# A Fourier mixing layer beside an MLP: rows copied once more inside DRAM by chunks, row tiles loaded right behind their stores, and another order of loads and VectorE work around blocks 2 and 3

## The chip, the cores and the metric

The kernel runs on one core of one Trainium2 chip. The metric is the device time of one execution in microseconds. A measurement has several executions; the time quoted is their median.

## The reference

The input x has 2048 rows (S) of 640 columns (D); the MLP has 1536 hidden columns (F). All is float32.

```
xn  = (x - mean) / sqrt(var + 1e-5)                      # each row
y_A = Cr @ (xn @ Wr.T) - Ci @ (xn @ Wi.T)                # DFT over columns, then rows; real part
y_B = gelu(xn @ w1 + b1, approximate) @ w2 + b2
out = x + y_A + y_B
```

Cr, Ci (2048 x 2048) and Wr, Wi (640 x 640) are inputs, the matrices of the transform.

## The kernel before, in words

**Precision.** Every operand of a matmul is split into a high part (ScalarE rounds it to fp32r, line 180) and a low part (VectorE subtracts, line 183). A product is three matmuls: high by high, high by low, low by high (lines 301 to 303, or 319 for the first layer of the MLP). A matmul of 128x128 by 128x512 comes every 0.227 us at full clock.

**Stages, in order of time.** The rows are cut into four blocks of 512 (t = 0 to 3) and the hidden columns into 12 units of 128.

1. Block 0 runs through the MLP in a loop over 12 units: `hidden` (15 matmuls), `gelu`, `output` (15 matmuls). Beside it, `background(i)` loads the rows of blocks 2 and 1 in chunks of 128, normalises them (`ln_stats`, `ln_scale`, `ln_apply`), stores them to the DRAM tensor `xs`, and loads them back in another layout (`load_z`, pieces of 640 bytes) for VectorE's 32x32 transposes. From these come the "forms" of a Winograd-like scheme (`make_forms`).
2. Blocks 1 and 2 go together: `pair(k)`, six times, multiplies combinations of W1 ("pieces", `make_pieces`) by combinations of the two blocks (`window`). The units of block 2 are kept in the DRAM tensor `gs` (`keep`). Beside each pair, `beside_pair(k, at)` does other work; `at` names a place within the pair, and the places come in the order 2, 5, 6, 3, 7, 4. This work finishes block 0, and prepares the matrices Wr and Wi for later (`load_w`, `turn_w`, `prep_w`, whose results are stored to `wits`).
3. The outputs of block 2, fourteen steps `p`: `output(g)`, then the split of the unit that is used two steps later (`split_unit`, its tile loaded by `load_unit` from `gs`), then `between(p)`. It finishes block 1 (`finish`, with adds on GpSimd), normalises chunks 12 to 15 (block 3) and loads them as `z3`, transposes and splits them (`transpose_z`, `prep_xt`), and prepares W1 anew (`prep_w1`, `load_w1`), in the order of the list `AGAIN`, into places that fall free (`open_place`).
4. Block 3 runs through the MLP as block 0 did. Beside it, `fourier_step(i)` builds the Fourier part's first operand from normalised rows: `build(k)`, k = 0 to 7, at i = k + 2. `load_xr(k)` brings the rows of a build: two tiles of 128 rows, each of 32 rows from each quarter of `xs`. For k below 4 the results (`xab`, 1,280 KB, and `xc`, 896 KB) are stored to DRAM too (`forms_ab`, `forms_c`).
5. The Fourier part: products over the sequence, then over the columns, to the end.

**Order.** The program is scheduled by hand: each engine runs its instructions in the order in which they are written, and waits where an operand or a place isn't ready. Nearly all DMAs are issued by SyncE's queue (SP), so a DMA that waits holds up all DMAs written behind it. A step's two waits on SP that matter here: `load_z` reads what `ln_apply` has stored, and `load_xr(k + 2)` writes rows that `build(k)` has read.

**Places.** `PLACES` names tiles that hold W1 and W2, then forms, then W1 again: "xab2" holds units 4 and 5 of W1, "xab3" units 6 and 7. In stage 3 "xab2" first holds `xo(1)` (the rows of x to which block 1's output is added) and "xab3" holds units 3 to 7 of `gs`.

Of the kernel before, what the change touches and what calls it, by code (L numbers as in the profile page):

```python
# [10 lines left out]
F32 = mybir.dt.float32  # L11
# [4 lines left out]
P = 128  # L16
# [9 lines left out]
def kernel(  # L26
# [65 lines left out]
        return stack.enter_context(tc.tile_pool(name=name, bufs=1, side=side, reuse_waits="tile"))  # L92

    dram = ctx.enter_context(tc.tile_pool(name="dram", bufs=1, space=bass.MemoryType.DRAM))
    xs = dram.tile([S, D], F32, name="xs")

    gs = dram.tile([NF, P, TB], F32, name="gs")

# [153 lines left out]
    def load_z(z, t):  # L252

        v = rows_of(xs, t)
        for q in range(Q):
            nc.sync.dma_start(z[q * B : (q + 1) * B], v[:, :, q * DQ : (q + 1) * DQ])
# [8 lines left out]
    W1, W2, w1r, w2r = {}, {}, {}, {}  # L265


    AGAIN = (0, 1, 2, 3, 8, 9, 10, 11, 4, 5, 6, 7)

    def load_w1(i, eng=nc.sync):  # L270

# [132 lines left out]
    def put_away():  # L404
        for f in stores:
            f()
        stores.clear()
# [157 lines left out]
    def load_xr(k):  # L565
        if k >= len(builds):
            return
        h, c = builds[k]
        xr[k] = []
        if k in (0, len(builds) - 1):  # L570
            n = 2 if k else 0
            A["xcp", n] = place(f"xc{n}{n + 1}", (P, 2, 2, 7 * P))
        for half in range(2):
            if k == len(builds) - 1:

                r = A["xcp", 2][:, 1, half, :D].bitcast(F32)
            else:
                r = row_places[:, (2 * k + half) % NC]
            s0 = (half * NS // 2 + h * NK + c) * B
            for q in range(Q):  # L580
                nc.sync.dma_start(r[q * B : (q + 1) * B], xs[q * SQ + s0 : q * SQ + s0 + B])  # L581
            xr[k].append(r)

    def build(k, what="abc"):
# [117 lines left out]
    def background(i):  # L702

        if i == 0:
            ln_apply(0)
            ln_apply(1)
            A["rows_b"] = zo_tile("rows_b", (P, NC, D))
            for c in range(2 * NC, 3 * NC):
                load_x(c, home=A["rows_b"])
        if i == 1:  # L710
            ln_apply(2)
            ln_apply(3)
            for c in range(NC, 2 * NC):
                load_x(c)
        if i == 2:
            for c in range(2 * NC, 3 * NC):
                ln_stats(c)
        if i == 3:
            ln_scale(NC)
            for c in range(2 * NC, 3 * NC):  # L720
                ln_apply(c)
            ln_stats(4)
            ln_stats(5)
        if i == 4:
            Z["b"] = zo_tile("z_b")
            load_z(Z["b"], 2)
            ln_stats(6)
            ln_stats(7)
            ln_scale(NC)
            for c in range(NC, 2 * NC):  # L730
                ln_apply(c)
        if i == 5:
            Z["a"] = as_z(row_places)
            load_z(Z["a"], 1)
        if i == 6:
            new_forms()
            make_forms("b", "vb0", "vb1", "ob0")
        if i == 7:
            make_forms("a", "ua0", "ua1", "va0", "va1", "oa0")
        if i >= 8:  # L740
            (ua, va), (ub, vb) = ((Z[k][:, :, : 2 * B], Z[k][:, :, 2 * B : 4 * B]) for k in "ab")
        if i == 8:
            add(ub, ub, ua, ALU.subtract)
            make_forms("b", "t10", "t11")
            add(vb, vb, ub, ALU.subtract)
        if i == 9:
            add(ua, vb, ua, ALU.subtract)
            add(va, va, vb, ALU.subtract)
            turn_x("t20", "b")
            turn_x("t21", "b")  # L750
            load_xo(0)
# [86 lines left out]
    def finish(t, *es):  # L838
        for e in es:
            add_block(xo[t], e, oacc[t][e], f"ot{t}_{e}", bias=b2c[:, e : e + 1])  # L840

    def store_sums(t):
        for k, (c0, c1) in enumerate(YCOLS):
            nc.sync.dma_start(ys[k][t], xo[t][:, :, c0:c1])
# [3 lines left out]
    def beside_pair(k, at):  # L848

        if k == 0:  # L850
            if at == 5:
                make_forms("a", "t30", "t31")
            if at == 6:
                make_forms("a", "t40", "t41")
                load_w(0, 0)
                load_w(1, 0)
            if at == 7:
                finish(0, 0, 1, 2)
            if at == 4:
                finish(0, 3, 4)  # L860
            return
        j = k - 1
        if at == 2 and k > 1:
            prep_w(j - 1, 2)
        if at == 5:
            if k > 1:
                put_away()
            else:
                store_sums(0)
        if at == 6:  # L870
            turn_w(0, j)
            turn_w(1, j)
        if at == 3:
            if k == 1:
                A["wst"], A["puts"] = zo_tile("wst", (P, 3, 2, 3 * P), F32R), 0
            prep_w(j, 0)
            if j + 1 < ND:
                load_w(0, j + 1)
                load_w(1, j + 1)
            put_away()  # L880
        if at == 7:
            prep_w(j, 1)
            if k == LASTK:
                prep_w(j, 2)
            put_away()
        if k == LASTK and at == 2:
            for i in range(3):
                load_unit(i)
        if k == LASTK and at == 4:
            for c in range(3 * NC, 4 * NC):  # L890
                load_x(c)
            load_xo(1, place("xab2", (P, NB, DQ), F32))
            A["gs"] = place("xab3", (P, 5, TB), F32)
            for i in range(3, 8):
                load_unit(i)

    units = {}

# [6 lines left out]
    def pair(k):  # L905
        x_, y_, z_ = (bank(5 + (k + m) % 3) for m in range(3))
        a1, a2, b1_, b2_ = (t * NF + 2 * k + m for t in (1, 2) for m in range(2))
        b = f"B{k % 2}"
        window(x_, "A", 0, "ua", True)
        u = term(a1, x_)  # L910
        window(y_, "A", 2, "va", True, ("A", 4, "oa0"))
        make_pieces(k + 1, *(("Bh", "Ah") if k else ("Ah",)))
        beside_pair(k, 2)
        put_out(0 if k else 5)
        u = unit(a1, y_, u, u)
        make_pieces(k + 1, *(("Al", "Bl") if k else ("Al",)))
        window(z_, "D", 2, "t1", True, (b, 2, "ob0"))
        zc = mr.tile([P, TB], F32, tag="zt", bufs=2, name=f"zc{k}") if k else early.tile([P, TB], F32, tag="w2r", bufs=3, name="zc0")
        split_unit(a1, u, lambda _: high(zc, z_))
        if k:  # L920
            make_pieces(k + 1, "+")
        beside_pair(k, 5)
        put_out(0 if k else 3)
        window(x_, "C", 0, "t2", False)
        v = term(b1_, x_)
        beside_pair(k, 6)
        put_out(2 if k else 0)
        window(z_, "C", 2, "vb", False, ("C", 4, "ob0"))
        make_pieces(k + 1, *(("Ch",) if k else ("Bh", "Bl", "+", "Ch")))
        keep(b1_, unit(b1_, z_, v, v))  # L930
        make_pieces(k + 1, "Cl")
        beside_pair(k, 3)
        put_out(4 if k else 0)
        window(x_, "D", 0, "t3", False)
        make_pieces(k + 1, "Dh")
        keep(b2_, unit(b2_, x_, zc))
        make_pieces(k + 1, "Dl")
        beside_pair(k, 7)
        put_out(10)
        window(x_, b, 0, "t4", False, (b, 2, "oa0"))  # L940
        gelu(a2, x_)
        beside_pair(k, 4)
        outputs.extend((g, e) for g in (a1, a2) for e in range(ND))

    def between(p):

        if p == 1:
            finish(1, 3, 4)
        if p == 2:
            ln_stats(12)  # L950
            ln_stats(13)
        if p == 3:
            ln_stats(14)
            ln_stats(15)
            ln_scale(NC)
            for c in range(3 * NC, 4 * NC):
                ln_apply(c)
            Z["z"] = zo_tile("z3")
            load_z(Z["z"], 3)
            new_xt(3)  # L960
        if p == 4:
            finish(1, 0, 1)
        if p == 5:
            finish(1, 2)
        if p == 6:
            store_sums(1)
        if p in (8, 9, 10):
            for j in ((0, 1), (2, 3), (4,))[p - 8]:
                transpose_z(f"x3{j}", Z["z"], j)
                prep_xt(f"x3{j}", j)  # L970
        if p == 11:
            load_xo(2)
        if p == 10:
            open_place(*PLACES[2])
        if p == 11:
            open_place(*PLACES[3])
        for n in {0: (0,), 2: (1,), 4: (2,), 5: (3,), 6: (4,), 7: (5, 6), 9: (7,), 10: (8,), 11: (9, 10), 12: (11,)}.get(p, ()):
            prep_w1(AGAIN[n], 2 * NF + n)
            load_w1(2 * NF + 3 + n)

# [607 lines left out]
```

## Time and profile before

| | |
|---|---|
| median of 3 runs | 890.05 us (886.58 to 891.08) |
| the profiled execution | 890.3 us, its span 888.5 us |
| mean granted TensorE clock | 0.987 |
| PE (matmul) busy | 857.1 us, 96%, 3718 matmuls |
| VectorE (DVE) busy | 683.8 us, 77% |
| ScalarE (ACT) busy | 365.5 us, 41% |
| GpSimd (POOL) busy | 22.8 us, 3% |
| DMA | 166.53 MB, mean 187 GB/s |
| row loads of load_xr | 56 + 8 of 80 KB |
| stage 3 (eleven outputs from 220.70 us) | until 270.93 us |
| first matmul of the Fourier part | 360.95 us |

In the profile, PE is TensorE's matmuls and PEld its weight loads, DVE VectorE, ACT ScalarE, POOL GpSimd, SP SyncE (SPq its queue of DMA issues). L581 is line 581 of the kernel. A group is written out<-in, with the program's tile names. Behind an instruction in a timeline, brackets give the engine's idle time before it and what ended that. "DMA share" is the mean busy share of the 16 DMA engines. A "gap" in the text is time in which PE ran no matmul.

### The profile page before, as it was taken

Reading aid. Unit: us, or ns where it says so; the run is one execution under the profiler, and the core shown is the slowest. Engines: PE = TensorE matmul, PEld = TensorE weight load, DVE = VectorE, ACT = ScalarE, POOL = GpSimd, SP = SyncE. Lnnn points to the kernel's source line nnn. Section 1 sums busy time; section 2 is a strip of 40 time slices with the busy share of each in tenths; the row PEclk is TensorE's granted clock in tenths of the full one; section 3 lists DMA queues with packets and bytes.
Section 4 is the critical chain, followed back from the end, with each engine's and each line's share of the span. In section 5 each row is a group of like instructions: output and inputs, shape, how many; then the busy total and the mean of one; then the engine's idle time right before and its main releaser. Section 6 shows DMA issues by size and latency. Waiting matters only on the chain.

```text
span 888.5 us, 10598 instructions
## 1 busy us (share of the span) xinstructions
PE 857.1 (96%) x3718; PEld 701.8 (79%) x3718; DVE 683.8 (77%) x892; ACT 365.5 (41%) x520; POOL 22.8 (3%) x22
## 2 busy tenths in 40 slices
PE   8999889999889999799999999999999999999996
PEld 6888678888667887588888888888888888888885
DVE  6787887775565456987989888888977988886586
ACT  5564465555335444543343444332232423223241
POOL 0000030000212000000000000000000000000000
PEclk9999899999899999999999999999999999999999
DMA  6995567778894996885865249946475779904364
GB/s 192 291 271 121 104 147 226 214 219 304 244 203 89 215 361 218 156 175 149 204 138 157 65 144 316 263 93 179 113 178 189 227 210 219 327 18 172 119 184 83
DMA packets 227765, 166.53 MB, mean 187 GB/s; under 512 B 84352, under 2 KB 197760, under 8 KB 227200
## 3 DMA queue, kind: packets, MB, share of 16 engines
q1 hardware_dynamic: 221760, 163.89, 68.5%
q10 hardware_dynamic: 5952, 1.97, 0.9%
q8 instruction: 29, 0.48, 0.2%
q14 instruction: 24, 0.20, 0.1%
HBM read 119.68 MB, written 46.14 MB: 187 GB/s over the span
## 4 chain that ended last, share of the span: by engine, by line
PE 75%; DMA 11%; DVE 7%; SPq 3%; ACT 2%; issue 2%; DVEq 0%; ACTq 0%
PE banks L303 24%; PE banks L302 24%; PE banks L301 24%; PE banks L319 3%; DMA row<-xs 2%; DMA forms_c<-xc 2%; DMA xs<-row 1%; DMA xab<-gs 1%; SPq L581 1%; DMA row<-in_A_x_dram 1%; DMA z<-xs 1%; DVE st L209 1%; DMA rows_b<-in_A_x_dram 1%; DVE as L183 1%; DMA raw<-in_A_dft_seq_re_dram 1%
## 5 line engine op out<-in xcount | busy, mean ns | idle before, releaser
L302 PE MATMUL banks<-as,xab 128*128 128x512 f32 x407 | 159.2, 391 | 3.5 <-DVE as L183 3.5
L301 PE MATMUL banks<-as,xab 128*128 128x512 f32 x407 | 159.1, 391 | 0.0
L303 PE MATMUL banks<-as,xab 128*128 128x512 f32 x407 | 159.0, 391 | 0.0
L180 ACT ACTIVATE as<-r 128x1024 fp32r<-128x1024 f32 x80 | 85.0, 1062 | 174.9 <-PE banks L303 148.7
L183 DVE TENSOR_TENSOR as<-r,as 128x1024 fp32r<-128x1024 f32 x80 | 97.2, 1216 | 40.3 <-ACT as L180 40.2
L302 PEld LDWEIGHTS banks<-as,xab 128*128 128x128 f32 x407 | 76.8, 189 | 20.5 <-DVE as L183 4.6
L301 PEld LDWEIGHTS banks<-as,xab 128*128 128x128 f32 x407 | 76.8, 189 | 16.2
L303 PEld LDWEIGHTS banks<-as,xab 128*128 128x128 f32 x407 | 76.7, 189 | 16.0
L301 PE MATMUL banks<-as,xc 128*128 128x512 f32 x224 | 87.1, 389 | 0.0
L302 PE MATMUL banks<-as,xc 128*128 128x512 f32 x224 | 87.1, 389 | 0.0
L303 PE MATMUL banks<-as,xc 128*128 128x512 f32 x224 | 87.1, 389 | 0.0
L180 ACT ACTIVATE as<-rt 128x1024 fp32r<-128x1024 f32 x32 | 34.0, 1063 | 69.8 <-PE banks L303 57.9
L319 PE MATMUL banks<-xt,xab 128*128 128x512 f32 x240 | 56.8, 390 | 0.2 <-ACT xt L180 0.2
L183 DVE TENSOR_TENSOR hs<-ab,hs 128x512 fp32r<-128x512 f32 x36 | 26.1, 725 | 37.1 <-ACT hs L180 37.1
L319 PEld LDWEIGHTS banks<-xt,xab 128*128 128x128 f32 x240 | 44.7, 188 | 10.3 <-ACT xt L180 1.3
L301 PE MATMUL banks<-hs,xc 128*128 128x512 f32 x120 | 48.2, 401 | 3.9 <-ACT hs L180 3.9
L303 PEld LDWEIGHTS banks<-as,xc 128*128 128x128 f32 x224 | 42.0, 188 | 8.8
L301 PEld LDWEIGHTS banks<-as,xc 128*128 128x128 f32 x224 | 42.0, 188 | 8.7
L302 PEld LDWEIGHTS banks<-as,xc 128*128 128x128 f32 x224 | 42.0, 188 | 8.7
L302 PE MATMUL banks<-hs,xc 128*128 128x512 f32 x120 | 48.1, 401 | 0.7 <-DVE hs L183 0.7
L303 PE MATMUL banks<-hs,xc 128*128 128x512 f32 x120 | 47.7, 397 | 0.0
L183 DVE TENSOR_TENSOR as<-rt,as 128x1024 fp32r<-128x1024 f32 x32 | 38.8, 1212 | 5.3 <-ACT as L180 5.3
(200 smaller groups left out, 1601.8 us busy)
## 6 DMA issues: line engine op xcount, KB each, us to landing
raw<-in_A_dft_seq_re_dram SPq DMA_DIRECT2D x64, 256.0 KB, 5.4
raw<-in_A_dft_seq_im_dram SPq DMA_DIRECT2D x64, 256.0 KB, 5.1
w1r<-in_B_w_dram SPq DMA_DIRECT2D x136, 80.0 KB, 2.6
wit<-wst SPq DMA_DIRECT2D x20, 384.0 KB, 3.2
ws<-wit SPq DMA_DIRECT2D x15, 384.0 KB, 5.1
forms_ab<-xab SPq DMA_DIRECT2D x4, 1280.0 KB, 5.3
xab<-wit SPq DMA_DIRECT2D x13, 384.0 KB, 4.4
row<-xs SPq DMA_DIRECT2D x56, 80.0 KB, 3.3
```

Of the source, the lines that this page charges most:

```text
L180: nc.scalar.activation(h, s, AF.Copy)
L183: nc.vector.tensor_tensor(l, s, h.bitcast(F32), op=ALU.subtract)
L209: nc.vector.bn_stats(st[:, h, :], xt[c][:, h * half : (h + 1) * half])
L301: nc.tensor.matmul(acc, wh, mh, start=first, stop=False, skip_group_check=goes_on)
L302: nc.tensor.matmul(acc, wh, ml, start=False, stop=False, skip_group_check=goes_on)
L303: nc.tensor.matmul(acc, wl, mh, start=False, stop=last, skip_group_check=goes_on)
L319: nc.tensor.matmul(acc, W1[i][:, a, j * P : (j + 1) * P], XT[j][:, b], start=n == 0, stop=n == len(steps) - 1)
L581: nc.sync.dma_start(r[q * B : (q + 1) * B], xs[q * SQ + s0 : q * SQ + s0 + B])
```

## The change

A second DRAM tensor `xn` holds the normalised rows in chunks: `xn[n]` has 128 rows, 32 from each quarter, as a build reads them. `by_chunks(t)` fills it from `xs` with one DMA inside DRAM for each block t (16 runs of 32 rows of 2,560 bytes). `load_xr` then takes a tile in one DMA instead of four. The copies of blocks 0 to 2 are issued in pairs 1 to 3, that of block 3 in step 5 of `between`.

In `background`, `load_z` of block 2 moves from step 4 to the end of step 3, and `load_z` of block 1 from step 5 to the end of step 4. In the first pair, all pieces of pair 1 but "Ah" and "Al" are made behind `keep(b2_)`, where some stood ahead of `keep(b1_)`. In the last pair the loads of x, of the units and of `xo(1)` get another order and other places. In `between`, several steps move, the transposes and splits of block 3 are spread over five steps instead of three, and the last four entries of `AGAIN` are exchanged.

```diff
+    xn = dram.tile([NS, P, D], F32, name="xn")
...
-    AGAIN = (0, 1, 2, 3, 8, 9, 10, 11, 4, 5, 6, 7)
+    AGAIN = (0, 1, 2, 3, 8, 9, 10, 11, 6, 7, 4, 5)
...  load_xr
-            s0 = (half * NS // 2 + h * NK + c) * B
-            for q in range(Q):
-                nc.sync.dma_start(r[q * B : (q + 1) * B], xs[q * SQ + s0 : q * SQ + s0 + B])
+            nc.sync.dma_start(r, xn[half * NS // 2 + h * NK + c])
...  background
             ln_stats(5)
-        if i == 4:
             Z["b"] = zo_tile("z_b")
             load_z(Z["b"], 2)
+        if i == 4:
             ln_stats(6)
             ln_stats(7)
             ln_scale(NC)
             for c in range(NC, 2 * NC):
                 ln_apply(c)
-        if i == 5:
             Z["a"] = as_z(row_places)
             load_z(Z["a"], 1)
...
+    def by_chunks(t):
+
+        nc.sync.dma_start(xn[:, t * B : (t + 1) * B], xs[t * TB : (t + 1) * TB].rearrange("(n r) d -> n r d", r=B))
...  beside_pair, at == 5
                 store_sums(0)
+            if k < NT:
+                by_chunks(k - 1)
...  beside_pair, at == 3
             put_away()
+            if k == LASTK:
+                load_x(12)
+                load_x(13)
         if at == 7:
             prep_w(j, 1)
             if k == LASTK:
+                A["gs"] = place("xab3", (P, 5, TB), F32)
+                for i in range(3, 6):
+                    load_unit(i)
                 prep_w(j, 2)
             put_away()
...
         if k == LASTK and at == 4:
-            for c in range(3 * NC, 4 * NC):
-                load_x(c)
+            load_x(14)
+            load_x(15)
+            for i in range(6, 8):
+                load_unit(i)
             load_xo(1, place("xab2", (P, NB, DQ), F32))
-            A["gs"] = place("xab3", (P, 5, TB), F32)
-            for i in range(3, 8):
-                load_unit(i)
...  pair
         window(z_, "C", 2, "vb", False, ("C", 4, "ob0"))
-        make_pieces(k + 1, *(("Ch",) if k else ("Bh", "Bl", "+", "Ch")))
+        if k:
+            make_pieces(k + 1, "Ch")
         keep(b1_, unit(b1_, z_, v, v))
-        make_pieces(k + 1, "Cl")
+        if k:
+            make_pieces(k + 1, "Cl")
         beside_pair(k, 3)
         put_out(4 if k else 0)
         window(x_, "D", 0, "t3", False)
-        make_pieces(k + 1, "Dh")
+        if k:
+            make_pieces(k + 1, "Dh")
         keep(b2_, unit(b2_, x_, zc))
-        make_pieces(k + 1, "Dl")
+        make_pieces(k + 1, *(("Dl",) if k else ("Bh", "Bl", "+", "Dh", "Ch", "Dl", "Cl")))
...  between
-        if p == 4:
-            finish(1, 0, 1)
         if p == 5:
+            finish(1, 0, 1)
+            by_chunks(3)
+        if p == 6:
             finish(1, 2)
-        if p == 6:
+        if p == 7:
+            transpose_z("x30", Z["z"], 0)
+        if 7 <= p < 7 + ND:
+            j = p - 7
+            if j + 1 < ND:
+                transpose_z(f"x3{j + 1}", Z["z"], j + 1)
+            prep_xt(f"x3{j}", j)
+        if p == 10:
             store_sums(1)
-        if p in (8, 9, 10):
-            for j in ((0, 1), (2, 3), (4,))[p - 8]:
-                transpose_z(f"x3{j}", Z["z"], j)
-                prep_xt(f"x3{j}", j)
-        if p == 11:
-            load_xo(2)
-        if p == 10:
-            open_place(*PLACES[2])
         if p == 11:
             open_place(*PLACES[3])
-        for n in {0: (0,), 2: (1,), 4: (2,), 5: (3,), 6: (4,), 7: (5, 6), 9: (7,), 10: (8,), 11: (9, 10), 12: (11,)}.get(p, ()):
+        if p == 12:
+            open_place(*PLACES[2])
+            load_xo(2)
+        for n in {0: (0,), 4: (1,), 5: (2,), 6: (3,), 7: (4,), 8: (5,), 9: (6,), 10: (7,), 11: (8,), 12: (9, 10), 13: (11,)}.get(p, ()):
             prep_w1(AGAIN[n], 2 * NF + n)
             load_w1(2 * NF + 3 + n)
```

More of the change, by code (lines that the diff above doesn't have):

```diff
@@ L960, in between @@
             new_xt(3)
-        if p == 4:
+        if p == 5:
             finish(1, 0, 1)
-        if p == 5:
+            by_chunks(3)
+        if p == 6:
             finish(1, 2)
-        if p == 6:
-            store_sums(1)
-        if p in (8, 9, 10):
-            for j in ((0, 1), (2, 3), (4,))[p - 8]:
-                transpose_z(f"x3{j}", Z["z"], j)
-                prep_xt(f"x3{j}", j)
-        if p == 11:
-            load_xo(2)
-        if p == 10:
-            open_place(*PLACES[2])
+        if p == 7:
[6 more added lines that the diff above has]
+        if p == 10:
+            store_sums(1)
         if p == 11:
             open_place(*PLACES[3])
-        for n in {0: (0,), 2: (1,), 4: (2,), 5: (3,), 6: (4,), 7: (5, 6), 9: (7,), 10: (8,), 11: (9, 10), 12: (11,)}.get(p, ()):
+        if p == 12:
+            open_place(*PLACES[2])
+            load_xo(2)
+        for n in {0: (0,), 4: (1,), 5: (2,), 6: (3,), 7: (4,), 8: (5,), 9: (6,), 10: (7,), 11: (8,), 12: (9, 10), 13: (11,)}.get(p, ()):
             prep_w1(AGAIN[n], 2 * NF + n)
```

## The prediction

> **What bounds the kernel now.** I read the page first, then the windows of 25 us, then the waits of PE, and last the timelines around each gap. The page gives PE as busy for 96% of the span, so only PE's gaps, and the half clock that follows some of them, can be won. Nearly all of them lie in six windows; from 400 to 800 us PE is 100% busy.
>
> ```profile
> 75.00:100.00 25.00, 21.13 (x83) 16.97 (x82) 23.21 (x36) 13.71 (x23) 0.00 (x0) 0.86 0.39 86
> 100.00:125.00 25.00, 22.34 (x92) 17.98 (x92) 18.97 (x30) 15.28 (x26) 6.91 (x5) 0.93 0.52 120
> ...
> 225.00:250.00 25.00, 20.44 (x75) 15.65 (x74) 15.07 (x27) 8.01 (x13) 7.94 (x5) 0.86 0.85 230
> 250.00:275.00 25.00, 22.13 (x91) 16.66 (x90) 13.98 (x21) 10.98 (x17) 0.00 (x0) 1.00 0.81 183
> ...
> 350.00:375.00 25.00, 20.71 (x85) 15.72 (x85) 22.31 (x36) 14.32 (x25) 0.00 (x0) 1.00 0.68 132
> 375.00:400.00 25.00, 22.66 (x93) 18.56 (x94) 21.89 (x19) 11.13 (x12) 0.00 (x0) 0.93 0.91 179
> ```
>
> The columns are the length, then busy us (instructions) of PE, PEld, DVE, ACT and POOL, then granted clock, DMA share, GB/s. A full window holds 112 matmuls (0.227 us each). Gaps of 3.87 (at 88.9), 2.66 (112.0), 3.87 (231.1) and 2.71 us (374.6) were each followed by some 3 to 7 us at clock 0.50; gaps up to 1.7 us were not.
>
> ```profile
> PE banks L301 <- ACT hs L180: 8.8, 6, 3.9
> PE banks L303 <- DVE w1f L183: 3.9, 1, 3.9
> PE banks L302 <- DVE as L183: 3.5, 2, 2.7
> PE banks L301 <- DVE ab L450: 2.7, 1, 2.7
> ```
>
> PE waits for ACT and DVE; what these wait for stands in ACT's timeline (in brackets its idle time before):
>
> ```profile
> 234.24 0.63 ACT L180 ACTIVATE hs<-xab 128x512 fp32r<-128x512 f32 x1 [12.09 <-DMA xab<-gs]
> ...
> 254.17 0.74 ACT L180 ACTIVATE as<-w1r 128x640 fp32r<-128x640 f32 x1 [8.38 <-DMA w1r<-in_B_w_dram]
> ...
> 318.92 0.53 ACT L604 ACTIVATE xab<-row 128x384 fp32r<-128x384 f32 x1 [5.46 <-DMA row<-xs]
> ```
>
> So the root is late loads, and SP's timeline says why:
>
> ```profile
> 308.23 9.80 SPq L581 DMA_DIRECT2D row<-xs  x8
> 318.12 0.37 SPq L986 DMA_DIRECT2D forms_ab<-xab  x1
> 318.59 0.38 SPq L987 DMA_DIRECT2D forms_c<-xc  x1
> 319.02 7.03 SPq L581 DMA_DIRECT2D row<-xs  x8
> 326.15 0.37 SPq L986 DMA_DIRECT2D forms_ab<-xab  x1
> ```
>
> Eight issues that take 0.42 us each when SP is free took 7 to 10 us. Of SP's 700 DMAs none is issued before the eighth DMA ahead of it has landed, and 33 go out within 0.06 us of that landing. A load cut in eight thus fills the whole allowance, and the next store stands behind it.
>
> **The change part by part.** All is counted against the profiled execution: 888.5 us of span, 890.3 us in all, 0.25 above the median of 890.05.
>
> *(1) One load for four (load_xr).* 64 DMAs of 80 KB become 16 of 320 KB; 48 issues of 0.42 us leave SP, and one build needs 4 places of the eight instead of 10. Build k can start when its hidden unit is through, that is at 299.8 + 6.8k (30 matmuls). It started at 299.8, 306.6, 318.9, 327.1, 335.6, 344.9, 351.6, 357.5: ten us late by the end. With the change the first four issues end some 6 us sooner, the two loads of raw land near 306 (now 312.7), and forms_ab(0) goes out at 303.6, when xab is ready, not at 306.75. Then bytes set the pace: 2,176 KB of forms landed 7.6 to 8.6 us after issue, less 2 us of latency 5.6 to 6.2, plus 640 KB of rows 1.6: 7.2 to 7.8 us a build against 6.8. Three such builds give 1.2 to 3 us of lateness at build 5, part of it won back after the last store; build 7 starts near 349 instead of 357.5, 8 to 9 us sooner. DVE then works without a pause (build, transposes, forms) to the form that PE waited for until 377.3; it is ready near 369, where PE without its gaps arrives at 368.6. What goes: gaps 1.57+0.22+1.70+0.22+0.75+2.71 = 7.2 and 1.6 of half clock (9 matmuls in 3.7 us), 8.8 together; what stays is up to 0.8. **I take -8.0** (bounds -6.5 and -8.8). From 381 on PE has no gap, so it all reaches the end.
>
> *(2) The units of g and the W1 tiles (beside_pair, between).* From 220.70 to 270.93 PE ran eleven outputs, 165 matmuls, worth 37.5 us: **12.8 us are lost**. units[3] was issued at 222.23 behind 8 loads of 320 KB (four of x; four of xo(1) in short pieces) and landed at 234.14; PE needed it split by 231. Moved ahead of them it is issued near 213.7 and lands by 217; x(12) and x(13) go out near 209. The norms of chunks 12 to 15, which waited behind the late unit, then end near 231 (now 241), their stores land near 234.7 (latency 3.6) and z3, with the 8.2 us that it has now, lands near 243. PE, an output of 3.4 us after another, needs unit 32 split by 247.9; behind z3 stand one transpose pair, one split and one W1 on DVE and ACT, done by 246.8: 1.1 us of margin. Five transposes and splits over five steps (2.9 us of DVE a step beside 3.4 of PE) take the place of two in a step, where PE lost 0.3 to 1.0 at each.
>
> Added here is by_chunks(3), 1.31 MB between z3 and the W1 load that unit 33 stands behind on ACT. No row is a copy from DRAM to DRAM. The nearest are the form stores, 1.31 MB at about 400 GB/s (3.3 us), and z in 640-byte pieces at 220 (6.3 us); a run of 80 KB is nearer the first but is read and written in DRAM, so I take 5. W1 then lands at 243.9+5+0.9 = 249.8 where 249.2 is needed: 0.6 lost, 0 to 1.9 between the ends. The Trainium skill (DMA: Bandwidth & Descriptors, "Latency and other measured facts") gives copies between DRAM tensors as 207 to 214 GB/s per direction, by which it would be an estimated 6.2 us and the loss 1.8; no run here shows it yet. With 0.5 for POOL's adds, which now fall beside the norms, **I take -11.7** (-9 to -12.8). store_sums(1), moved from step 6 to 10, has until xab2 opens at 12; load_xo(2) issues near 257, lands 8 us on, and is first added to near 269.5: 4 us of cover, and each us beyond would hold DVE's transposes behind POOL.
>
> *(3) Pieces of pair 1 (pair, k = 0).* Of 112.0 to 118, 4.5 us are lost: the add of zc at 113.83 stood on DVE behind Bl, five adds and Cl, and PE's window "t4" waited for it. Without them it is done at 111.4 and "t4" starts at 112.0. But the pieces now stand ahead of the three biases on ACT, so gelu(a2) reads its bank near 117.7 to 118.4, and pair 1's third window, which writes that bank, waits 1.1 us from 117.4. Its window after that waits for the copy zc, behind transposes that POOL's adds of 1.26 us pace: 124.6, where PE comes at 123.2. Before it began at 126.58. **I take -2.0** (0 to -3.5).
>
> *(4) Tiles of z behind their stores (background).* load_z(2) still waits for stores that land at 51.57, so it goes out at 51.6 as now. Behind it on SP now wait W1(10), W2(8) and the stores of chunks 4 to 7; by the rule of eight these go out at 56.8 to 60.1 (now 53.6 to 55.8). The queue loses 1.7 us empty until 53.4, and the same bytes end near 64.8 instead of 64.3. z1 lands near 73 (now 72.48), so DVE, idle before it, starts the forms 0.5 later and the gap at 88.9 stays. **+0.5** (-4, the gap itself, if W1(11) and W2(9), now ahead of z1, were what held it; +2 if the stores come later still).
>
> *(5) by_chunks(0) to (2).* Each follows stores on SP where the queue falls empty (148.3 to 150.5, 168.0 to 169.7); what stands behind is W1 for the next pair, with over 6 us of cover. **+0.2** (0 to 2); without that cover, their excess over it.
>
> Sum: -8.0 - 11.7 - 2.0 + 0.5 + 0.2 = -21.0; 890.3 - 21.0 - 0.3 = **869 us**.
>
> **The rivals.** *The W1 tiles stay late.* z3, the copy and W1 share one queue, and margins are 1 us. For it: DMA share 0.81 to 0.85 there; against: the byte counts above. If the chain is 3 us later, a gap of some 3 us brings the half clock back (3 more): 875.
>
> *The form stores set the pace.* If forms and rows take 9 us a build, as between 335.6 and 344.9, the builds win only the start: -4 instead of -8, 873. Against it: these 9 us hold eight issues behind one another.
>
> *Slower: the copies run on few DMA engines.* Sixteen move 424 GB/s at share 1.00 (window 312 to 315), so one moves 26.5 and copies 1.31 MB in 49 us. SP stops at the ninth DMA behind it. In the pairs up to about 12 us is covered; beyond that, three copies cost 20 us or more each, and the fourth about 40: over 960. With four engines the fourth copy alone costs 7 us; with two (25 us) the gain of 21 is used up, which is where it decides. For it: nothing here shows a copy of 16 runs; against: loads of 32 rows use the engines well enough to land 80 KB in 2.0 us. The Trainium skill (same page, "Why a DMA increments its semaphore by 16 and not by 1") says the engines are the largest number up to 16 that divides the slowest dimension of both sides, which is 16 here; no run here shows it for such a copy.
>
> *No difference.* The loads arrive as said, but each wait passes to another late load (z3, rows behind forms): below 4.5 us in all, about 887. Against it: separate stages would each have to fail.
>
> **How the numbers follow.** Forecast 0.62, W1 late 0.14, stores set the pace 0.12, few engines 0.08, no difference 0.04. Faster by over 0.5% (4.5 us, about what a measurement can tell): 0.88; within: 0.04; slower: 0.08. All bounds at their best give -29, 861; at their worst -11.5, 878.5; both milder rivals lie inside, and together they reach 881. Range 861 to 882.
>
> **What would show it.** Right: row loads x16 of 320 KB; builds 6.8 to 7.8 us apart with build 7 near 336 (349 less the 13 gained before); no ACT wait for xab<-gs; the gaps at hs between 256 and 268 gone; eleven outputs in 38 to 40 us; clock 1.00 where it was 0.86 (231) and 0.93 (375); the gap at "w1f" still there, near 4 us. Wrong: copies that take over 7 us to land; an ACT wait for w1r; a gap above 2 us at "as" when the Fourier part starts.

## The result, and the profile after

The changed kernel takes 879.93 us (median; 875.36 to 880.90), against 888.61 us for the kernel before in the same comparison: a ratio of 0.9888, 95% interval 0.9855 to 0.9922. Its profiled execution took 878.27 us with a span of 876.3, so 12.2 us of span went where 21.0 were forecast.

First the windows of 25 us of the changed kernel (length, then busy us of PE, PEld, DVE, ACT and POOL, clock, DMA share, GB/s):

```profile
75.00:100.00 25.00, 20.86 (x82) 16.54 (x81) 23.20 (x35) 13.61 (x23) 0.00 (x0) 0.86 0.50 115
100.00:125.00 25.00, 23.09 (x100) 18.18 (x98) 18.81 (x30) 15.13 (x27) 6.70 (x5) 1.00 0.50 117
125.00:150.00 25.00, 24.13 (x105) 19.63 (x106) 20.05 (x44) 13.29 (x28) 0.00 (x0) 1.00 0.98 282
150.00:175.00 25.00, 23.17 (x96) 18.70 (x95) 16.28 (x39) 12.94 (x30) 0.00 (x0) 0.93 0.83 261
...
225.00:250.00 25.00, 25.00 (x112) 20.72 (x111) 17.52 (x34) 8.33 (x13) 7.40 (x5) 1.00 0.98 225
250.00:275.00 25.00, 21.89 (x88) 17.38 (x88) 14.57 (x22) 12.74 (x20) 0.00 (x0) 0.93 0.89 237
275.00:300.00 25.00, 22.91 (x99) 18.02 (x99) 9.70 (x13) 9.56 (x17) 7.25 (x5) 1.00 0.75 170
...
350.00:375.00 25.00, 25.00 (x112) 20.67 (x112) 23.57 (x28) 12.25 (x18) 0.00 (x0) 1.00 1.16 211
375.00:400.00 25.00, 25.00 (x112) 20.71 (x111) 21.90 (x19) 10.32 (x10) 0.00 (x0) 1.00 0.56 126
```

Three windows that had lost time are full now, 225 to 250 and the two from 350 to 400. But 125 to 175, where PE had had no gap, lost matmuls (105 and 96 of 112), with a DMA share of 0.98 in the first. PE's waits:

```profile
PE banks L305 <- DVE w1f L185: 4.1, 1, 4.1
PE banks L303 <- ACT zc L182: 3.7, 3, 1.8
PE banks L303 <- ACT hs L182: 2.7, 1, 2.7
PE banks L303 <- DVE ot L380: 2.1, 3, 1.1
```

The waits of 8.8 us for hs, 3.5 for "as" and 2.7 for ab are gone or small; those for zc (in the pairs) and for ot (block 3's outputs, behind block 2's sums) are new. ACT's timeline names what stands behind the largest:

```profile
157.76 0.62 ACT L182 ACTIVATE wst<-row 128x256 fp32r<-128x256 f32 x2 [4.07 <-DMA wit<-wst]
...
252.19 0.63 ACT L182 ACTIVATE xt<-ztx 128x512 fp32r<-128x512 f32 x1 [10.37 <-DVE ztx L262]
...
256.77 0.74 ACT L182 ACTIVATE as<-w1r 128x640 fp32r<-128x640 f32 x1 [2.28 <-DMA w1r<-in_B_w_dram]
```

In the pairs ACT waited 4.07 us (at most 1.58 before) until a store of wit had landed and its buffer was free. At 252 it waited for DVE's transposes of z3, and DVE for z3 itself. SP's timeline:

```profile
146.19 0.63 SPq L843 DMA_DIRECT2D xn<-xs  x1
150.15 0.33 SPq L835 DMA_DIRECT2D gs<-ab  x1
...
222.99 4.46 SPq L373 DMA_DIRECT2D xab<-in_A_x_dram  x4
227.55 3.92 SPq L913 DMA_DIRECT2D g<-gs  x1
231.56 1.81 SPq L281 DMA_DIRECT2D w1r<-in_B_w_dram  x4
234.72 1.76 SPq L913 DMA_DIRECT2D g<-gs  x2
237.46 2.51 SPq L228 DMA_DIRECT2D xs<-row  x4
243.29 1.91 SPq L258 DMA_DIRECT2D z<-xs  x4
...
311.06 0.98 SPq L581 DMA_DIRECT2D row<-xn  x2
```

and the page's line for the copies (KB each, median us to landing):

```profile
xn<-xs SPq DMA_DIRECT2D x4, 1280.0 KB, 7.8
```

A build's two row loads in the Fourier part now pass SP in 1.0 to 2.2 us where its eight had taken 7 to 10 (the four loads of the last two builds take 5.7). The four copies landed after 7.64, 8.90, 6.36 and 7.97 us. The four row tiles were normalised by 234.4, but their stores left SP at 237.46 to 239.56.

To place the time, both traces are cut at the same matmuls (PE runs the same 3718 in the same order). **Loss** is the time from the start of one such matmul to the next less 0.2273 us for each between; a little below zero is rounding.

| stretch (times after) | before | after | moved | forecast |
|---|---|---|---|---|
| forms, gap at "w1f" (72 to 93) | 4.4 | 4.7 | +0.3 | +0.5 |
| pair 0 and the start of 1 (93 to 125) | 6.6 | 5.2 | -1.4 | -2.0 |
| pairs 1 to 5 (125 to 224) | 0.0 | 4.4 | +4.4 | +0.2 |
| eleven outputs (224 to 267) | 12.7 | 5.2 | -7.6 | -11.7 |
| block 3's first outputs (267 to 286) | 0.1 | 2.9 | +2.8 | 0 |
| builds, Fourier start (286 to 380) | 10.3 | -0.2 | -10.6 | -8.0 |

Together -12.1; all the rest adds -0.1.

### The profile page after: what moved, and what is told of

The parts are those of the page before. It is cut to its first block, busy times and chain, and to the rows that moved or that the text cites. A ratio compares the mean times of both kernels' runs of the same rounds, so it can differ in the third digit from the quotient of the medians.

```text
span 876.3 us, 10521 instructions
## 1 busy us (share of the span) xinstructions
PE 852.8 (97%) x3718; PEld 700.2 (80%) x3718; DVE 683.4 (78%) x892; ACT 364.8 (42%) x520; POOL 22.1 (3%) x22
## 4 chain that ended last, share of the span: by engine, by line
PE 67%; DMA 4%; SPq 2%; DVE 1%; POOL 1%; issue 0%; ACT 0%; POOLq 0%; DVEq 0%; ACTq 0%
PE banks L303 21%; PE banks L304 21%; PE banks L305 21%; PE banks L321 3%; DMA xab<-in_A_x_dram 1%; DMA w1r<-in_B_w_dram 1%; DMA xo<-in_A_x_dram 1%; SPq L281 1%; DMA wit<-wst 1%; POOL xo L382 0%; SPq L847 0%; SPq L373 0%; DMA xs<-row 0%; SPq L258 0%; DVE as L185 0%
## 5 line engine op out<-in xcount | busy, mean ns | idle before, releaser
L321 PEld LDWEIGHTS banks<-xt,xab 128*128 128x128 f32 x240 | 44.7, 188 | 10.3 <-ACT xt L182 1.3
L303 PE MATMUL banks<-hs,xc 128*128 128x512 f32 x120 | 47.0, 392 | 2.1 <-DVE ot L380 2.1
L305 PE MATMUL banks<-hs,xc 128*128 128x512 f32 x120 | 46.7, 389 | 0.0
L304 PE MATMUL banks<-hs,xc 128*128 128x512 f32 x120 | 46.7, 389 | 0.0
```

The source lines that it names most:

```text
L303: nc.tensor.matmul(acc, wh, mh, start=first, stop=False, skip_group_check=goes_on)
L304: nc.tensor.matmul(acc, wh, ml, start=False, stop=False, skip_group_check=goes_on)
L305: nc.tensor.matmul(acc, wl, mh, start=False, stop=last, skip_group_check=goes_on)
L321: nc.tensor.matmul(acc, W1[i][:, a, j * P : (j + 1) * P], XT[j][:, b], start=n == 0, stop=n == len(steps) - 1)
```

## The experiments

Each was timed beside the kernel before. Losses are read from each one's own profile by the same cuts:

| kernel | forms | pair 0/1 | pairs | outputs | block 3 | Fourier start | ratio to before, 95% interval |
|---|---|---|---|---|---|---|---|
| before | 4.4 | 6.6 | 0.0 | 12.7 | 0.1 | 10.3 | |
| changed | 4.7 | 5.2 | 4.4 | 5.2 | 2.9 | -0.2 | 0.9888 (0.9855 to 0.9922) |
| e11, changed again | 6.9 | 5.4 | 4.6 | 5.8 | 2.8 | -0.2 | 0.9892 (0.9869 to 0.9916) |
| e1, loads alone | 3.9 | 5.5 | 2.5 | 16.3 | 0.0 | -0.2 | 0.9959 (0.9940 to 0.9978) |
| e2, order alone | 4.4 | 4.7 | 0.6 | 5.0 | 1.2 | 7.2 | 0.9927 (0.9900 to 0.9955) |
| e3, no copies | 35.7 | 4.7 | 0.5 | 16.6 | 1.6 | -0.2 | 1.0283 (1.0254 to 1.0312) |
| e4, copies later in the pair | 8.4 | 3.1 | 7.0 | 7.6 | 2.0 | 0.1 | 0.9916 (0.9888 to 0.9944) |
| e5, copies on ACT's queue | 6.1 | 5.4 | 10.7 | 8.7 | 0.8 | -0.2 | 0.9980 (0.9961 to 0.9999) |
| e6, copies in quarters | 6.5 | 4.7 | 8.4 | 5.5 | 2.5 | 1.4 | 0.9937 (0.9915 to 0.9959) |
| e7, xo earlier | 7.2 | 3.1 | 5.3 | 4.6 | 2.4 | 0.3 | 0.9878 (0.9845 to 0.9911) |
| e8, pieces and z undone | 6.4 | 6.2 | 3.6 | 7.4 | 2.4 | -0.2 | 0.9878 (0.9846 to 0.9911) |
| e9, copies in quiet places | 6.9 | 4.2 | 0.4 | 7.1 | 0.3 | 5.6 | 0.9893 (0.9868 to 0.9918) |
| e10, the same and xo earlier | 7.1 | 5.4 | 0.8 | 5.7 | 0.1 | 8.7 | 0.9890 (0.9864 to 0.9916) |
| e12, last copy behind xo(2) | 6.7 | 4.7 | 0.4 | 5.2 | 0.1 | -0.2 | 0.9783 (0.9759 to 0.9808) |

The column "forms" runs from 3.9 to 8.4 (e3 aside) although most of these kernels do not differ from the changed one there. It goes with the landing of z1, block 1's tile for the forms: 71.9 to 72.7 us in before, changed, e1 and e2, which lost 3.9 to 4.7, and 74.3 to 76.7 in the others, which lost 6.1 to 8.4. What made z1 late in those is open, so nothing of the change is read from this column.

**What do the copies cost, and the parts alone?** e1 is the kernel before with by_chunks as in the change and

```
+    xn = dram.tile([NS, P, D], F32, name="xn")
-            for q in range(Q):
-                nc.sync.dma_start(r[q * B : (q + 1) * B], xs[q * SQ + s0 : q * SQ + s0 + B])
+            nc.sync.dma_start(r, xn[half * NS // 2 + h * NK + c])
+            if k < NT:
+                by_chunks(k - 1)        # beside_pair, at 5
+            by_chunks(3)                # between, step 5
```

> The kernel before with the copies and the one load for four alone; loads of units, of W1 tiles and of z stay as before. Theory (the copies cost the pairs 4.4 us and the last copy holds W1 back): the gap at the Fourier start goes (-8.8), pairs 1 to 5 (from pair 1's C2 window, 94.1 us before) take 97 to 99 us, and the W1 tiles behind the fourth copy come some 3 us later than before, so 886 to 890 us in the profiled execution. Rival (copies harmless, the pairs are slower for another part of the change): pairs 94 us, only the -8.8 remains, 880 to 882.

Profiled execution: 883.95 us, between the two ranges. The Fourier start gained 10.6 us where 8.8 were expected; the pairs lost 2.5 us, less than the 3 to 5 expected, and the outputs 3.6 more than before, where ACT now waited 9.27 and 3.37 us for w1r (8.38 and 0.44 before). Both losses stand where the theory has them.

e2 is the changed kernel less these same lines.

> The changed kernel without the copies, with rows loaded in four pieces as before. Theory: pairs 1 to 5 take 94 us again (-4.4), ACT's wait of 2.28 us for w1r goes with the gap of 2.67 us and its half clock (-3.4), the late builds come back (+8.8): 877 to 881. Rival (copies harmless): only the +8.8 shows, pairs stay at 98 us, 885 to 888.

Profiled execution: 879.4 (the fastest of its runs; their median is 883.56). The pairs lost 0.6 instead of 4.4, and ACT waited at most 1.87 us for wit:

```profile
154.55 0.62 ACT L181 ACTIVATE wst<-row 128x256 fp32r<-128x256 f32 x2 [1.87 <-DMA wit<-wst]
```

So the three copies in the pairs cost 3.8 us: the theory holds there. It fails in the outputs: without the fourth copy the wait for w1r was gone, but the loss stayed (5.0 against 5.2), since DVE still waited for z3 (5.54 us, and 4.70 in the changed kernel). The fourth copy cost 1.6 us, in block 3's outputs. The late builds came back with 7.2 us. The two parts add up: the ratios of e1 and e2 multiply to 0.9886.

**Can the copies be spared?** e3 stores each row tile once, straight into the order of chunks:

```
-        nc.sync.dma_start(xs[c * P : (c + 1) * P], xt[c])
+        t, n = c // NC, c % NC * (P // B)
+        nc.sync.dma_start(xn[n : n + P // B, t * B : (t + 1) * B], xt[c])
-        v = rows_of(xs, t)                                  # load_z
+        v = xn[:, t * B : (t + 1) * B].rearrange("n r d -> r n d")
```

> The changed kernel with each normalised row tile stored once, straight into the order of chunks (4 runs of 32 rows), and z read from there: no copy inside DRAM, one load for four kept. Theory: pairs back to 94 us (-4.4), the wait for w1r in the last stretch gone (-3.4): 869 to 872. Rival (copies harmless): 877 to 879. If stores in four runs land later than 3.6 us, z1 and with it the gap near 89 us grows by as much.

Profiled execution: 916.3. The pairs lost 0.5, as expected, but each group of four stores took so long that all that waits for z was late by 11 to 17 us (DVE waited 16.82, 15.99 and 16.50 us for the three tiles of z, and 0, 4.54 and 4.70 us in the changed kernel). The windows of e3 while SP waits for those of block 2 and of block 1 to land:

```profile
60.00:70.00 10.00, 9.67 (x43) 7.61 (x42) 6.34 (x10) 5.38 (x9) 0.00 (x0) 1.00 0.25 86
...
90.00:100.00 10.00, 7.92 (x28) 6.01 (x27) 0.22 (x1) 0.00 (x0) 0.00 (x0) 0.84 0.29 102
```

A DMA share of 0.25 is four engines of sixteen, and 86 GB/s is below the 106 that four of them can move at the 26.5 each of the forecast. A store of four runs of 32 rows thus ran on four engines. This is the mechanism of the rival "few engines"; the change's copies, of sixteen runs, do not have it: the third copy of e9, e10 and e12, beside which least ran, landed after 6.0 to 6.9 us, 191 to 218 GB/s, and two copies issued 0.7 us apart near 86 us (2.62 MB) had both landed after 10.0 to 10.6 us, 248 to 263 GB/s. The Trainium skill (DMA: Bandwidth & Descriptors, "Why a DMA increments its semaphore by 16 and not by 1") has the rule that gives four engines here and sixteen for the copies; the trace agrees as far as these rates tell.

**Is it the place in the queue, or the bytes?** e4 moves the three copies:

```
-            if k < NT:
-                by_chunks(k - 1)      # at 5
...
             put_away()
+            if k < NT:
+                by_chunks(k - 1)      # at 7
```

> The changed kernel with the three copies in the pairs issued some 11 us later, behind the stores of the window at 7, where SP has nothing due for about 8 us; the fourth copy stays. Theory (what costs is the place: stores of wit and W1 behind the copy): pairs 1 to 5 take 94 to 95.5 us, 874 to 875. Rival (bytes: the copy takes its time from other transfers wherever it stands): pairs stay near 98 us, 877 to 879.

Profiled execution: 884.25, pairs 7.0. Neither was right: it got worse. The last three stores of wit in a group now followed the copy in SP's queue and landed 8.8 to 11.1 us after their issue (3.1 to 5.1 in the changed kernel), none of them before the copy. So the place does matter: what stands right behind a copy pays for it.

e5 was to take the queue away as a cause: `nc.scalar.dma_start` for `nc.sync.dma_start` in by_chunks.

> The changed kernel with its four copies issued by ACT instead of SP. Theory (what is behind a copy in SP's queue lands after it: stores of wit then keep their buffers, ACT waits, zc is late): with the copies in a queue of their own ACT's wait of 4.07 us for wit falls to 2 us, PE's gap of 1.83 us for zc with its half clock goes (-3.7), 874 to 875.5 in the profiled execution. Rival (bytes: a copy takes the DMA engines' time whatever the queue): the wait stays over 3 us and PE loses 2 to 4 us as before, 877 to 879.

Profiled execution: 887.75, pairs 10.7, far slower than either range. The copies themselves landed sooner (6.15 to 7.35 us), and ACT's wait for wit did not fall:

```profile
157.29 0.61 ACT L182 ACTIVATE wst<-row 128x256 fp32r<-128x256 f32 x2 [4.11 <-DMA wit<-wst]
```

This looks like the rival's answer, but SP's and ACT's DMAs show another reason:

```profile
142.67 12.08 SPq L281 DMA_DIRECT2D w1r<-in_B_w_dram  x4
154.85 2.89 SPq L426 DMA_DIRECT2D wit<-wst  x5
```
```profile
147.11 0.54 ACTq L843 DMA_DIRECT2D xn<-xs  x1
```

The copy landed at 154.42. SP's last W1 load had stood since 144.19 and went out at 154.44; the stores of wit behind it landed within 2.4 to 3.2 us, but were issued some 10 us late. In this trace all DMAs, SP's and ACT's, take eight semaphores (counters that a landing raises) in turn, and none is issued before the DMA that had its semaphore last has landed. This load's semaphore was that of the copy, which ACT had issued only at 147.11. The same came at 177.35 and 177.37. So the rule of eight counts ACT's DMAs too, and e5 did not free SP from the copies. That a copy slows transfers of another queue shows elsewhere in e5: three of the four loads of z3, issued on SP up to 1.4 us behind the fourth copy on ACT's queue, landed 7.8 to 9.7 us after their issue (4.7 to 6.6 in the changed kernel). How the 3.8 us of the pairs divide between waiting behind a copy and sharing the engines with it, the runs do not show.

e6 cuts each copy into four of 8 rows a chunk, `xn[:, t * B + 8 * m : t * B + 8 * m + 8]`, at windows 5, 6, 3 and 7, and those of tile 3 behind four W1 steps.

> The changed kernel with each copy cut into four of 16 runs of 20 KB (8 rows of each chunk), one at each of four windows of a pair, and those of tile 3 behind four W1 steps. Theory of the queue: each quarter holds what is behind it for about 2 us, less than the slack, so the wit wait falls to 2.5 us and the gap for zc goes: 874 to 875.5. Rival (bytes): the same 2.6 MB read and written in the pairs delay the stores as much in sum, PE loses 2 to 4 us in pairs 2 and 3: 877 to 879. A third way: quarters of 20 KB runs land slower than 2.2 us each, more gaps than now, over 880.

Profiled execution: 885.08, pairs 8.4. The third way came: the quarters in the pairs landed 3.9 to 5.6 us after issue, not 2.2, and ACT waited 3.85, 3.88 and 4.05 us for wit, PE 1.7 to 2.0 us for zc in three pairs. Cutting a copy in four thus costs more. As the quarters took more than the slack that the theory of the queue gave them, this run does not decide between that theory and the bytes.

**Why was z3 late?** e7:

```
             if k == LASTK:
...
                 prep_w(j, 2)
+                load_xo(1, place("xab2", (P, NB, DQ), F32))     # at 7
...
-            load_xo(1, place("xab2", (P, NB, DQ), F32))         # at 4
-            if p in (0, 1, 2, 8):
-                load_unit(min(8 + p, NF - 1))
+            if p in (0, 4, 5, 8):
+                load_unit({0: 8, 4: 9, 5: 10, 8: 11}[p])
-            load_xo(2)                                          # between, step 12
+            load_xo(2)                                          # step 11
```

> The changed kernel with the four loads of xo(1) ahead of x(14) and x(15) instead of behind them, units 9 and 10 loaded behind z3, and xo(2) loaded one output earlier. Theory (the stores of the last four row tiles were ready at 232.7 to 234.4 but went out at 237.5 to 239.6, each when the eighth DMA ahead, of xo(1), had landed): they go out 3 to 4 us sooner, z3 lands near 247.5 instead of 251.3, PE loses 1.5 to 2.5 us there instead of 5.25, and 1 us instead of 2.9 at block 3's outputs: 872.5 to 874.5 in the profiled execution. Rival (bytes: the queue is full from 217 to 240 and the order only moves the lateness on to x(14) and x(15)): z3 within 1 us of 251.3, 876 to 878.

Profiled execution: 879.61, outputs 4.6 instead of 5.2. The stores now left as soon as DVE had the rows:

```profile
237.46 2.18 DVE L227 TENSOR_SCALAR row<-row,mv 128x640 f32<-128x640 f32 x4
```
```profile
238.10 1.89 SPq L228 DMA_DIRECT2D xs<-row  x4
243.24 1.91 SPq L258 DMA_DIRECT2D z<-xs  x4
```

but x(15) landed 9.5 us after the first of the eleven outputs began, 4.8 in the changed kernel, so DVE applied the norms 3.8 us later. Counted from there z3 landed at 26.3 instead of 27.3: the rival is right, the order only moves the lateness on. What the outputs lose goes with this landing in the versions with the new order of W1 (e3 aside): 4.6 to 5.7 us where z3 landed 26.3 to 27.4 us after the first output, 5.8 to 7.6 at 28.1 to 28.9, and 8.7 at 30.2 (e5).

**The two small parts.** e8 puts pair 1's pieces back (`make_pieces(k + 1, *(("Ch",) if k else ("Bh", "Bl", "+", "Ch")))` and so on) and the loads of z back to steps 4 and 5.

> The changed kernel with pair 1's pieces and the two loads of z put back where they were before. Theory: the first window of pair 0's end waits 2.7 us for the add of zc again and runs at half clock, the waits of 0.92 and 1.44 us in pair 1 go; PE loses 6.6 us between 93 and 125 us instead of 5.2; the gap near 89 us is 3.9 instead of 4.1: +1.2, 879 to 880. Rival (the pieces' new place makes the pairs behind late as well): pairs 2 and 3 lose 1 us or less instead of 3.8, 876 to 877.

Profiled execution: 881.5; pair 0/1 lost 6.2, the pairs 3.6 (4.4 and 4.6 with the pieces moved). The three kernels with the pieces in their old place lost 5.5 to 6.6 us in pair 0/1, the others 3.1 to 5.4. The gaps alone are 2.7 us against 2.3 to 2.4; the rest is mostly how long the half clock lasted. So the new place gains something, but these runs do not price it, and the ratio does not differ from the changed kernel's. The rival falls.

**Where the DMA engines are idle.** The changed kernel's DMA share is 0.12 from 80 to 90 us and 0.30 from 280 to 290. e9:

```
             add(vb, vb, ub, ALU.subtract)
+            by_chunks(0)                     # background, step 8
         if i == 9:
+            by_chunks(1)
...
             if at == 5:                      # pair 0
+                by_chunks(2)
...
+        if p == 13:                          # between
+            by_chunks(3)
```

> The changed kernel with its copies where the DMA engines are least used: tiles 0 and 1 behind the last W1 load near 83 us (share 0.12 from 80 to 90), tile 2 near 101 us (share 0.28), tile 3 behind xo(2) near 275 us (share 0.30 from 280 to 290). Theory (a copy costs DMA engine time, some 7 us where the pairs already use 0.65 to 0.8 of it; its queue and its place within the pairs do not matter): pairs 1 to 5 lose under 1 us instead of 4.4, the last stretch and block 3's outputs lose 6.3 instead of 8.1; 872 to 874 in the profiled execution where nothing else differs. Rival (any copy of 1.31 MB costs PE some us wherever it stands, here by a late xo(0) and rows behind it): what the pairs win is lost between 93 and 125 us, 877 to 879.

Profiled execution: 880.5, outside both ranges. The pairs lost 0.4, with pair 0/1 no worse (4.2): the theory holds for the three copies. The outputs and block 3's together lost 7.4 us where 6.3 were expected. And the ratio did not move, for the fourth copy was issued later than meant:

```profile
283.00 3.67 SPq L849 DMA_DIRECT2D ys<-xo  x3
286.72 1.87 SPq L845 DMA_DIRECT2D xn<-xs  x1
294.58 1.78 SPq L581 DMA_DIRECT2D row<-xn  x4
```

It stood behind the stores of block 2's sums, and the first row loads behind it; the late builds were back (5.6 us). e10 is e9 with the lines of e7.

> The same places for the copies, with xo(1) ahead of x(14) and x(15), units 9 and 10 behind z3 and xo(2) one output earlier as well. Theory of bytes: the order gains at most 1 us over the run with the copies in quiet places alone: 871 to 874. Rival (the order was worth its 4 us and the copy in the pairs had hidden it): 868 to 870.

Profiled execution: 883.49, above both ranges: outputs 5.7 instead of 7.1, and the same fault at the Fourier start (8.7). e11 is the changed kernel once more, beside these two.

> The changed kernel as it is, once more beside these two on the same chip: 878 to 880, 0.987 to 0.991 of the kernel before; PE loses 4 to 5.5 us in pairs 1 to 5. If it loses under 2 us there this time, the loss is the chip's scatter and not the copies.

Profiled execution: 881.41, pairs 4.6: the loss there is no scatter. Nor is that of block 3's outputs.

e12 is e10 with `by_chunks(3)` at step 12 instead of 13, ahead of those stores.

> The run before (copies in quiet places, and the order of xo, units 9 and 10) with one change: the copy of tile 3 is issued behind xo(2) near 272 us, not behind the sums of block 2 near 287 us. Theory: there it held SP and the row loads by 8 us (landed 294.95, the first rows 297.8), so the late builds came back; now it lands by 285, the rows by 294.5, and the 8.8 us that PE lost between 320 and 380 us go: 872 to 874.5 in the profiled execution, 0.980 to 0.985 of the kernel before. Rival (the row loads stay late for another reason, the queue being full from 290 to 330): 3 us or more of the 8.8 stay, over 876.

Profiled execution and median 872.36 us, before 891.39 beside it: 0.9783 (0.9759 to 0.9808). The copy now went out ahead of the stores of block 2's sums, the row loads ten us sooner than in e9, and the Fourier start lost nothing; the rival falls.

```profile
269.85 0.59 SPq L845 DMA_DIRECT2D xn<-xs  x1
280.91 3.65 SPq L849 DMA_DIRECT2D ys<-xo  x3
284.66 3.27 SPq L581 DMA_DIRECT2D row<-xn  x4
```

Behind the program's start, e12's waits of PE above 1.2 us are the old gap and three small ones:

```profile
PE banks L305 <- DVE w1f L185: 4.2, 1, 4.2
...
PE banks L303 <- ACT hs L182: 1.7, 1, 1.7
PE banks L321 <- ACT as L182: 1.6, 1, 1.6
PE banks L303 <- ACT zc L182: 1.5, 1, 1.5
```

It is the fastest version, 1.1% below the changed kernel (0.9783 by e11's 0.9892, each against the kernel before in its own comparison).

## Why the prediction was right about the sign and wrong about the size

The time lies in the range of 861 to 882, but near its slow end, and it is there partly by luck: of the six stretches three moved beyond their bounds, two for the worse and one for the better, and a fourth was not in the sum. Two of the three signs of being wrong came (copies over 7 us, an ACT wait for w1r).

**(1) One load for four** was right in mechanism and a little small: -10.6 against -8.0, past its best end of -8.8. Build 7 began 9.2 us sooner where 8 to 9 were forecast (at 346.8, not 357.5, of which 1.5 had been gained before), and none of the 0.8 us that might stay did. The rest was mis-sized: the loss of 10.3 us before, less the 7.2 of gaps, leaves 3.1 where 1.6 was counted. The nine matmuls at half clock are 1.6 of it; the starts right beside the gaps, 0.1 to 0.3 us late each, were left out. The rival "stores set the pace" is out: the stores of forms_c landed every 6.7 to 6.8 us. (8.6 us less 2 is 6.6, not 6.2, so a build could have taken 8.2 by the forecast's own rows; one took 8.3, the others 5.9 to 6.8.)

**(2) Units and W1 tiles**: -7.6 against -11.7, below its smaller bound. The step that failed is "their stores land near 234.7". Counted from the first of the eleven outputs (220.70 in the forecast, 223.99 now), the rows were normalised after 10.4 us, as forecast (10.3):

```profile
232.18 2.19 DVE L227 TENSOR_SCALAR row<-row,mv 128x640 f32<-128x640 f32 x4
```

But then SP stood on xo(1) and what followed it: the first three stores went out 0.06 to 0.07 us after the eighth DMA ahead of each had landed, and the last landed at 243.28, 19.3 us after that point where 14.0 was forecast. The steps behind kept the forecast's pace (8.0 us for z3, forecast 8.2), so z3 came after 27.3 us, not 22.3. The rule of eight had been read from the same trace, but it was not applied to loads 9 and 10 of g and to the stores. e7 shows that applying it would have saved 1 us, not 5: the queue is full there (DMA share 0.95 to 1.06 from 210 to 240), and what is put ahead makes x(14) and x(15) late. The rival "W1 late" had the price nearly right, with a gap of 2.67 us at hs and half clock behind it, but named the wrong load: w1r was late by 2.28 us, and without that wait (e2) the loss stayed, for z3 was later. In this stage, then, the wait passed on to another load, as the rival "No difference" has it.

**(3) Pieces of pair 1**: -1.4 against -2.0; the waits of 0.92 and 1.44 us that were foreseen in pair 1 came. **(4)** +0.3 against +0.5, with z1 at 72.70 where 73 was forecast; that the same kernel had it at 74.96 in e11 shows how little this term can be told.

**(5) The copies in the pairs**: +4.4 against +0.2, beyond the bound of 2; 3.8 of it is the copies' (e2). Two things were mis-sized. The price of a copy was put at 5 us, and those of the changed kernel took 6.4 to 8.9; the ones beside which least ran took 6.0 to 6.9. By the Trainium skill (DMA: Bandwidth & Descriptors, "Latency and other measured facts"), whose 207 to 214 GB/s stand for row pitches that do not slow the copy, it would have been an estimated 6.2, nearer to these than the row of form stores that the sum used. (The other row, 1.31 MB of z in 6.3 us, is 208 GB/s, not 220.) And "where the queue falls empty" was read from gaps of 2 us in SP's timeline; the cover named, of 6 us, was that of W1. What had no such cover were the stores of wit: ACT waited for them even without copies. A wait of 1.6 us (e12) cost PE nothing, 2.2 (e11) cost it a gap of 0.8, 4.1 one of 1.8. And the DMA share of the pairs, 0.71 to 0.81 by windows of 25 us in the kernel before (125 to 200 us), said that 7 us more in each 20 would fill them.

**What was not in the sum**: block 3's outputs, +2.8. xo(2) was forecast to land by 265 with 4 us of cover; it was issued at 271.66, behind W1 tiles and the stores of block 1's sums, and landed at 280.47, 13.4 us after the start of this stretch (267.12). Over the versions the loss goes with that distance: 0 to 0.3 us up to 10.7 us, 0.8 at 11.3 (e5), 1.2 at 11.7 (e2, without any copy), 1.6 at 12.0 (e3), and 2.0 to 2.9 from 12.4 to 13.4. By these figures the cover is an estimated 10.5 us; in e2 the new order alone used it up, and the copy ahead of xo(2) added to the loss.

## What to carry to other kernels

A transfer that "fits into an idle moment of the queue" is to be costed by the share of the DMA engines over the whole loop that it falls into, and against the shortest cover of what is behind it, stores that free a buffer included. Here moving it within that loop, cutting it, or changing its queue did not help; moving it to where the engines were idle (shares of 0.12 and 0.28), or where nothing due stood behind it, did. Where a load that three engines wait for is late, follow it back through every transfer that shares its queue before giving its gain to the first one that can be moved.

## What was not expected of the hardware

The clock after a gap is not told by the gap's length. In the changed kernel a gap of 1.83 us at 166.41 was followed by nine matmuls in 3.9 us at half clock:

```profile
166.41 0.71 PE L303 MATMUL banks<-xab,w1f 128*128 128x512 f32 x1 [1.83 <-ACT zc L182]
166.92 0.63 PE L304 MATMUL banks<-xab,w1f 128*128 128x512 f32 x1
167.35 0.63 PE L305 MATMUL banks<-xab,w1f 128*128 128x512 f32 x1
```

while e7 and e8 lost only 0.3 us beside the gap after 1.92 and 1.84 us at the same matmul, and e7 as little after 2.73 at "w1f". The Trainium skill (TensorE: Matmul & The Clock Gate, "Part 1: The HAM clock gate") has a window of 3.4 us that runs free of the kernel, which would make the outcome a matter of where a gap falls; the trace fits that, but its rule of an idle window of 3.4 us does not fit a drop after 1.83.

VectorE's split of 512 elements took 0.69 us alone and 1.77 beside POOL's adds (POOL ran them at 241.30 and 244.42, for 1.87 and 1.78 us):

```profile
235.60 0.69 DVE L185 TENSOR_TENSOR hs<-xab,hs 128x512 fp32r<-128x512 f32 x1
...
241.95 1.77 DVE L185 TENSOR_TENSOR hs<-xab,hs 128x512 fp32r<-128x512 f32 x1
```

Open are why z1 landed 2 to 4 us later in most of the kernels that do not differ up to there, and how z3 could land sooner: in every version of the new order it came 26.3 us or more after the first of the eleven outputs, which lost 4.6 us or more.
